# Who makes the sums of the activations' quarters, VectorE or GpSimd, in a kernel whose order a planner sets

## The chip, the cores and the metric

The kernel runs on one core of one Trainium2 chip. The metric is the device time of one execution in microseconds (us). The core's engines are called here as the profile calls them: PE (TensorE, matmuls; PEld is its weight load), DVE (VectorE), ACT (ScalarE), POOL (GpSimd) and SP (SyncE, which issues the DMA transfers).

## The reference

Eight batches of attention between 512 tokens and 32 states in 8 heads of 64, in both directions, give 512 + 32 rows of width 512 a batch. A feed-forward layer with a hard-swish follows on all 4352 rows. All arithmetic is fp32.

```python
scores = scale * x @ state.T;  a = softmax(scores);   xread = a @ state
scores2 = scale * state @ x.T; a2 = softmax(scores2); sread = a2 @ x
x = concat([xread, sread], axis=2)        # (8, 8, 544, 64) -> 4352 x 512
h = x @ w_in                              # 512 x 2048
g = h * clip(h + 3, 0, 6) / 6
out = g @ w_out                           # 2048 x 512
```

## The kernel before, in words

**Split products.** The PE multiplies in fp32r, which keeps fewer digits than fp32. An operand is therefore split into a high and a low half: ACT copies it into an fp32r tile (the high half, line 379), DVE subtracts that from the original (the low half, line 380), and each product is three matmuls (high by high, high by low, low by high).

**Units and steps.** The hidden width of 2048 is cut in 16 blocks `f` of 128. The work runs in two sweeps, blocks 0 to 7 and blocks 8 to 15. In each sweep there are nine units: one for the 512 tokens of each of the eight batches, and a ninth for all 256 state rows. A unit has eight steps, one a block. `first` (its matmuls stand on line 988, into a bank `ps_h`; there are two such banks) makes one block of `h`; ACT adds 3 and clips below (line 1159, tile `G`), DVE clips above and multiplies (line 1161). The first sweep's `second` multiplies that by `w_out` and adds up in four PSUM banks `acc`. Each unit also needs `wprime` (line 604), which folds a batch's states into `w_in`; its results are split as well (tiles `wp_hi`, `wp_lo`, at some units `raw`).

**Seven products in place of eight.** In the second sweep the units of batches 1 to 7 (units 10 to 16) run the second product by a seven-product scheme, in `seconds(k, t)`. The 512 tokens are two halves `q`, each two groups `r` of 128; the eight blocks are four pairs `p`, each two blocks `i`. For one `t`, which is one (q, p), the left operand is a 2 by 2 arrangement of quarters (i, r), each 128 x 128. Four sums of quarters are made (tile `g`, name `s_of(m)`): (0,1)+(1,1), (0,0)-(0,1), then the first less (0,0), and (1,0) less that. They are split into a pair of tiles `tmp` of 128 x 512; the four quarters themselves are split into `g_hi`, `g_lo` of 128 x 512. Seven products, of three matmuls each, go to the four banks on line 1075. Fifty-six `t` run so: 7 units of 8. `combine` makes the right operands' sums once, from `w_out`, on DVE. At the end of each half `q` the banks are put together: ACT and DVE evict them, and four additions (line 1098: two of 128 x 256 in the tile `tops`, two of 128 x 512 into `ot`) finish the output rows.

The names that the change touches are these two lines; `G_` puts an instruction on POOL, `V` on DVE, and the numbers are what the planner takes it to cost:

```python
SUMS, SUM_ENGINE, SUM_COST = G_, nc.gpsimd, 0.4
ADDS, ADD_ENGINE, ADD_COST = G_, nc.gpsimd, (0.7, 1.3)
```

**What sets the order.** Nothing is issued as the code meets it. Every instruction group is handed to `Plan` with its engine, a cost, and what it reads and writes. `Plan.order` then simulates all engines and the DMA queue with those costs and, among what is ready, takes the one with the lowest number in the table `RANKS`. A DMA counts as landed after its size over a rate, 1.4 us and a further allowance `late`. Each engine executes its list strictly in that order.

Of the kernel before, what the change touches and what calls it, by code (L numbers as in the profile page):

```python
# [10 lines left out]
F32 = mybir.dt.float32  # L11
# [268 lines left out]
def tile_state_attention_then_hardswish_ffn(  # L280
# [13 lines left out]
    P = 128  # L294
# [687 lines left out]
    def product(ps, terms, start=True, stop=True):  # L982
# [3 lines left out]
        for (ah, al), (bh, bl) in terms:  # L986
            for l, r in ((ah, bh), (ah, bl), (al, bh)):
                nc.tensor.matmul(ps, l, r, start=start and k == 0, stop=stop and k == n - 1)  # L988
                k += 1

    first_of = {}
    whole_of = {}

    def whole(k, p):

# [465 lines left out]
```

## Time and profile before

| | |
|---|---|
| median of 3 runs | 665.23 us (664.82 to 666.5) |
| profiled execution | 665.26 us, of which the profile's span is 663.5 us |
| PE busy | 642.4 us, 97% |
| DVE busy | 483.2 us, 73% |
| ACT busy | 337.3 us, 51% |
| POOL busy | 190.1 us, 29% |
| granted PE clock | full in the stretches from 0 to 640 us |

Busy is the time in which an engine executes at least one instruction. POOL's share is low only over the whole span: it does next to nothing until the seven-product units begin at about 395 us. Matmuls overlap one another, so one that is listed with 0.28 us can be followed by the next after 0.12 us.

### The profile page before, as it was taken

Reading aid. Unit: us, or ns where it says so; the run is one execution under the profiler, and the core shown is the slowest. Engines: PE = TensorE matmul, PEld = TensorE weight load, DVE = VectorE, ACT = ScalarE, POOL = GpSimd, SP = SyncE. Lnnn points to the kernel's source line nnn. Section 1 sums busy time; section 2 is a strip of 40 time slices with the busy share of each in tenths; the row PEclk is TensorE's granted clock in tenths of the full one; section 3 lists DMA queues with packets and bytes.
Section 4 is the critical chain, followed back from the end, with each engine's and each line's share of the span. In section 5 each row is a group of like instructions: output and inputs, shape, how many; then the busy total and the mean of one; then the engine's idle time right before and its main releaser. Section 6 shows DMA issues by size and latency. Waiting matters only on the chain.

```text
span 663.5 us, 11542 instructions
## 1 busy us (share of the span) xinstructions
PE 642.4 (97%) x4383; PEld 516.1 (78%) x4383; DVE 483.2 (73%) x799; ACT 337.3 (51%) x591; POOL 190.1 (29%) x287
## 2 busy tenths in 40 slices
PE   8999999999999999999999999999999999999997
PEld 7446776877777777777886788988888979889896
DVE  4989798988979668686589447666866577776753
ACT  4856445555545544535356336455555455545442
POOL 0000000000000000000000017777876588687732
PEclk9999999999999999999999999999999999999999
DMA  9975795867777549243013033232131312240012
GB/s 296 281 157 157 151 207 123 236 112 216 163 205 160 153 88 254 32 127 91 7 68 127 38 131 127 100 93 98 46 127 56 135 54 79 96 160 33 33 65 63
DMA packets 147007, 82.00 MB, mean 124 GB/s; under 512 B 124808, under 2 KB 134536, under 8 KB 144776
## 3 DMA queue, kind: packets, MB, share of 16 engines
q1 hardware_dynamic: 146808, 81.01, 44.7%
q8 instruction: 34, 0.56, 0.4%
q10 hardware_dynamic: 144, 0.26, 0.1%
q14 instruction: 21, 0.17, 0.1%
HBM read 50.84 MB, written 26.74 MB: 117 GB/s over the span
## 4 chain that ended last, share of the span: by engine, by line
PE 64%; POOL 11%; DVE 11%; ACT 4%; SPq 4%; DMA 3%; issue 3%; DVEq 0%; POOLq 0%; ACTq 0%
PE acc L988 23%; PE ps_h L988 22%; PE acc L1075 9%; POOL g L1045 9%; PE ps_s L604 2%; DVE tmp L380 2%; PE ps_s L988 2%; POOL ot L1098 2%; ACT tmp L379 2%; DMA raw<-in_moe_w_in_dram 2%; PE acc L1209 2%; SPq L917 1%; SPq L591 1%; DVE g_lo L380 1%; PE ps_h L604 1%
## 5 line engine op out<-in xcount | busy, mean ns | idle before, releaser
L1045 POOL TENSOR_TENSOR g<-G 128x128 f32<-128x128 f32 x112 | 67.8, 618 | 428.2 <-DVE G L1161 397.8
L988 PE MATMUL acc<-w_out_hi,g_hi 128*128 128x512 f32 x288 | 114.4, 397 | 0.0
L988 PE MATMUL acc<-w_out_hi,g_lo 128*128 128x512 f32 x288 | 112.2, 390 | 0.9 <-DVE g_lo L380 0.9
L1075 PE MATMUL acc<-w_out_hi,tmp 128*128 128x256 f32 x448 | 111.4, 286 | 1.7 <-DVE tmp L380 1.3
L988 PE MATMUL acc<-w_out_lo,g_hi 128*128 128x512 f32 x288 | 112.4, 390 | 0.0
L1174 ACT ACTIVATE g<-ps_h,three 128x512 f32<-128x512 f32 (+1 forms) x88 | 57.2, 650 | 78.4 <-PE ps_h L988 61.0
L988 PE MATMUL ps_h<-aT_hi,wp_hi 128*128 128x512 f32 (+1 forms) x232 | 85.8, 370 | 3.2 <-DVE wp_lo L380 1.7
L1075 PEld LDWEIGHTS acc<-w_out_hi,tmp 128*128 128x128 f32 x448 | 82.6, 191 | 7.0 <-issue 2.5
L988 PE MATMUL ps_h<-aT_lo,wp_hi 128*128 128x512 f32 (+1 forms) x232 | 83.9, 362 | 0.2 <-DVE aT_lo L380 0.2
L1176 DVE SCALAR_TENSOR_TENSOR g<-g,ps_h 128x512 f32<-128x512 f32 (+1 forms) x88 | 55.7, 635 | 39.0 <-ACT g L1174 38.2
L988 PE MATMUL ps_h<-aT_hi,wp_lo 128*128 128x512 f32 (+1 forms) x232 | 83.6, 360 | 0.0
L380 DVE TENSOR_TENSOR g_lo<-g,g_hi 128x512 fp32r<-128x512 f32 (+1 forms) x84 | 54.7, 655 | 21.9 <-ACT g_hi L379 20.2
L379 ACT CAST g_hi<-g 128x512 fp32r<-128x512 f32 (+1 forms) x84 | 48.5, 579 | 41.4 <-PE acc L988 30.9
L988 PEld LDWEIGHTS acc<-w_out_hi,g_hi 128*128 128x128 f32 x288 | 54.1, 188 | 19.4 <-issue 7.8
L380 DVE TENSOR_TENSOR tmp<-g,tmp 128x512 fp32r<-128x512 f32 x56 | 46.2, 833 | 28.8 <-ACT tmp L379 27.3
L988 PEld LDWEIGHTS acc<-w_out_hi,g_lo 128*128 128x128 f32 x288 | 54.1, 188 | 12.8 <-DVE g_lo L380 1.4
L1075 PE MATMUL acc<-w_out_lo,tmp 128*128 128x256 f32 x224 | 63.4, 283 | 0.0
L988 PEld LDWEIGHTS acc<-w_out_lo,g_hi 128*128 128x128 f32 x288 | 54.1, 188 | 10.9 <-DVE w_out_lo L496 0.3
L1159 ACT ACTIVATE G<-ps_h,three 128x512 f32<-128x512 f32 x56 | 38.4, 689 | 44.9 <-PE ps_h L988 44.7
L1161 DVE SCALAR_TENSOR_TENSOR G<-G,ps_h 128x512 f32<-128x512 f32 x56 | 37.9, 683 | 30.4 <-ACT G L1159 30.1
L379 ACT CAST tmp<-g 128x512 fp32r<-128x512 f32 x56 | 34.2, 619 | 47.1 <-POOL g L1045 45.8
L988 PEld LDWEIGHTS ps_h<-aT_hi,wp_hi 128*128 128x128 f32 x232 | 43.8, 189 | 13.9 <-DVE wp_lo L380 2.4
(152 smaller groups left out, 1304.0 us busy)
## 6 DMA issues: line engine op xcount, KB each, us to landing
part<-ot SPq DMA_DIRECT2D x8, 1024.0 KB, 5.0
ot<-part SPq DMA_DIRECT2D x8, 1024.0 KB, 6.2
raw<-in_x_dram SPq DMA_DIRECT2D x112, 64.0 KB, 2.9
xb<-in_x_dram SPq DMA_DIRECT2D x28, 256.0 KB, 4.3
out_dram<-ot SPq DMA_DIRECT2D x14, 512.0 KB, 3.2
raw<-in_moe_w_out_dram SPq DMA_DIRECT2D x11, 511.8 KB, 5.9
raw<-in_moe_w_in_dram SPq DMA_DIRECT2D x8, 511.0 KB, 4.5
raw<-raw SPq DMA_DIRECT2D x112, 32.0 KB, 2.0
```

The source lines that it names most:

```text
L379: S_(cost, rank, lambda: nc.scalar.copy(hi(), src()), reads, [writes[0]])
L380: V(cost, rank, lambda: nc.vector.tensor_tensor(lo(), src(), hi().bitcast(F32), op=ALU.subtract), [*reads, writes[0]], [writes[1]])
L604: nc.tensor.matmul(out[u][cols, :], made["stT", b][rows, cols], moving(q)[rows], start=True, stop=True,)
L988: nc.tensor.matmul(ps, l, r, start=start and k == 0, stop=stop and k == n - 1)
L1045: SUMS(SUM_COST, rank - 2.5, lambda m=m, a=a, b=b, op=op, of=of: SUM_ENGINE.tensor_tensor(s_of(m), of(a), of(b), op=op), g_keys + [(*s_key ...
L1075: nc.tensor.matmul(out, left(a, l), right(b, r), start=p == 0 and z == 0 and y == 0, stop=p == FPS // 2 - 1 and y == 2, skip_group_check=True)
L1098: add = lambda wide, out, a, b, reads, writes: ADDS(ADD_COST[wide], rank, lambda: ADD_ENGINE.tensor_tensor(out(), a(), b(), op=ALU.add), r ...
L1159: S_(0.68, n - 1.5, lambda: nc.scalar.activation(g(), bank(ps), AF.Relu, bias=three), [ps], [g_key], after)
L1161: V(0.63, n - 1.5, lambda: nc.vector.scalar_tensor_tensor(g(), g(), 6.0, bank(ps), op0=ALU.min, op1=ALU.mult), [ps], [g_key])
L1174: S_(cost + 0.05, rank, lambda: nc.scalar.activation(g(), bank(ps)[:, :width], AF.Relu, bias=three), [ps], [g_key])
L1176: V(cost, rank, lambda: nc.vector.scalar_tensor_tensor(g(), g(), 6.0, bank(ps)[:, :width], op0=ALU.min, op1=ALU.mult), [ps], [g_key])
L1209: nc.tensor.matmul(bank(acc), made["g_hi", n][:, js], plain_out[f][1](), start=opens, stop=closes)
```

## The change

The four sums of quarters move from POOL to DVE. The second of them, now (0,1) less (0,0), with the opposite sign, is written over the quarter (0,1), which no product uses by itself. It is then split along with the quarters, in the tile that already held a split of (0,1), so the sums' own tile has three parts instead of four and its split is 128 x 384 instead of 128 x 512. The split of the quarters now waits for that subtraction. The right operand gets the opposite sign too. POOL keeps the additions on the banks' results. The planner's costs are new for the sums and the additions, its allowance for DMA is 2.0 instead of 3.0, some loads may be issued earlier, and the table RANKS is new.

```diff
 RANKS = [int(k) for k in """
-159 160 158 211 208 311 209 59 207 58 232 60 233 55 226 57 234 205 206 54 56 309 215 231 307 567 308 219 214 306 216
...
-    def Q(rank, size, do, reads=(), writes=(), after=(), pieces=128, cost=0.46, late=3.0):
+    def Q(rank, size, do, reads=(), writes=(), after=(), pieces=128, cost=0.46, late=2.0):
...
-        for m, a, less in ((0, (0, 1), (0, 0)), (2, (1, 1), (0, 1)), (1, (1, 1), 0), (3, (1, 0), 1)):
+        for m, a, less in ((0, (0, 1), (0, 0)), (2, (0, 1), (1, 1)), (1, (1, 1), 0), (3, (1, 0), 1)):
...
-        s_all = lambda: get(s_key, lambda: gp.tile([P, S], F32, name="g"))
+        s_all = lambda: get(s_key, lambda: gp.tile([P, S], F32, name="g"))[:, : 3 * P]
         s_of = lambda m: s_all()[:, m * P : (m + 1) * P]
         for m, a, b, op, reads in (
-            (0, (0, 1), (1, 1), ALU.add, ()), (2, (0, 0), (0, 1), ALU.subtract, ()),
-            (1, 0, (0, 0), ALU.subtract, (0,)), (3, (1, 0), 1, ALU.subtract, (1,)),
+            (0, (0, 1), (1, 1), ALU.add, ()), ((0, 1), (0, 1), (0, 0), ALU.subtract, (0,)),
+            (1, 0, (0, 0), ALU.subtract, (0,)), (2, (1, 0), 1, ALU.subtract, (1,)),
         ):
             of = lambda c: s_of(c) if isinstance(c, int) else quarter(*c)
-            SUMS(SUM_COST, rank - 2.5, lambda m=m, a=a, b=b, op=op, of=of: SUM_ENGINE.tensor_tensor(
-                s_of(m), of(a), of(b), op=op), g_keys + [(*s_key, r) for r in reads], [(*s_key, m)])
-        s_keys = [(*s_key, m) for m in range(4)]
+            sum_of[k * FPS + t, m] = SUMS(SUM_COST, rank - 2.5, lambda m=m, a=a, b=b, op=op, of=of: SUM_ENGINE.tensor_tensor(
+                of(m), of(a), of(b), op=op), g_keys + [(*s_key, r) for r in reads],
+                [(*s_key, m)] if isinstance(m, int) else [("G", (k, p), "less", q)],
+                [sum_of[k * FPS + t - 1, m]] if (k * FPS + t - 1, m) in sum_of else [])
+        s_keys = [(*s_key, m) for m in range(3)]
...
         split(rank - 2, a_half["hi"], a_half["lo"], lambda: whole(k, p)[:, :, 2 * q * P : 2 * (q + 1) * P],
-              g_keys, a_keys)
-        split(rank - 1.5, s_half["hi"], s_half["lo"], s_all, s_keys, half_keys)
+              [*g_keys, ("G", (k, p), "less", q)], a_keys)
+        split(rank - 1.5, s_half["hi"], s_half["lo"], s_all, s_keys, half_keys, 0.5)
...
             (((0, 0), (0, 0)), (1, 1)),
-            ((2, 2),),
-            (((1, 0), (1, 0)), (3, (1, 1))),
+            (((0, 1), 2),),
+            (((1, 0), (1, 0)), (2, (1, 1))),
             (((1, 1), 3), (0, 0)),
...
-    SUMS, SUM_ENGINE, SUM_COST = G_, nc.gpsimd, 0.4
-    ADDS, ADD_ENGINE, ADD_COST = G_, nc.gpsimd, (0.7, 1.3)
+    SUMS, SUM_ENGINE, SUM_COST = V, nc.vector, 0.24
+    ADDS, ADD_ENGINE, ADD_COST = G_, nc.gpsimd, (0.85, 1.45)
...
-        first_of[n] = T(1.95 if plain(k, c) else 1.37 if b < B else 1.45, n, run, reads, [ps], after)
+        first_of[n] = T(1.95 if plain(k, c) else 1.37 if b < B else 1.45, n, run, reads, [ps],
+                        after + ([first_of[n - 3]] if n > 2 else []))
...
-            at(n - 2, sread_split, k, n - 3)
+            at(n - 2, lambda k=k, n=n: sread_split(k, n - 3, [first_of[n - FPS]]))
...
-            at(n - 5, lambda k=k, n=n: again(k, n - 6, [first_of[n - 6]]))
+            at(n - (10 if k == B + 1 else 5), lambda k=k, n=n: again(k, n - 6, [first_of[n - (11 if k == B + 1 else 6)]]))
```

The built programs have the same number of instructions on PE (3745), ACT (578) and SP (395). POOL goes from 292 to 68, DVE from 801 to 1025. On PE 336 matmuls change an operand (`tmp` for `g_hi` or `g_lo`), none its size.

The first place is POOL's list in the middle of the seven-product units, before the change, with the sums (line 1045) and the additions of one half's end (line 1098):

```order
L1045 TENSOR_TENSOR g<-G 128x128 x2
L1045 TENSOR_TENSOR g<-g,G 128x128
L1045 TENSOR_TENSOR g<-G,g 128x128
L1098 TENSOR_TENSOR tops<-tops 128x256
L1098 TENSOR_TENSOR ot<-ot,tops 128x512
L1098 TENSOR_TENSOR tops<-tops 128x256
L1098 TENSOR_TENSOR ot<-ot,tops 128x512
L1045 TENSOR_TENSOR g<-G 128x128 x3
L1045 TENSOR_TENSOR g<-g,G 128x128
L1045 TENSOR_TENSOR g<-G,g 128x128
```

A stretch of POOL's list after the change (the additions now stand on line 1100):

```order
L1100 TENSOR_TENSOR tops<-tops 128x256
L1100 TENSOR_TENSOR ot<-ot,tops 128x512
L1100 TENSOR_TENSOR tops<-tops 128x256
L1100 TENSOR_TENSOR ot<-ot,tops 128x512
L1100 TENSOR_TENSOR tops<-tops 128x256 x2
L1100 TENSOR_TENSOR ot<-ot,tops 128x512 x2
```

All sums are gone from it: what was queued behind additions is on another engine.

The second place is DVE's list before the change at unit 14, where the folded weights of that unit (`wp_lo` and `raw`, from `ps_h` and `ps_s`) are split behind the low halves of two sums (`tmp`):

```order
L1161 SCALAR_TENSOR_TENSOR G<-G,ps_h 128x512
L380 TENSOR_TENSOR tmp<-g,tmp 128x512
L1161 SCALAR_TENSOR_TENSOR G<-G,ps_h 128x512
L1092 SCALAR_TENSOR_TENSOR ot<-acc_4830,ot 128x512
L380 TENSOR_TENSOR g_lo<-G,g_hi 128x512
L380 TENSOR_TENSOR tmp<-g,tmp 128x512
L1095 SCALAR_TENSOR_TENSOR ot<-acc_4858,ot 128x256
L380 TENSOR_TENSOR wp_lo<-ps_h,wp_hi 128x512 x2
L380 TENSOR_TENSOR raw<-ps_s,raw 128x512 x2
L1161 SCALAR_TENSOR_TENSOR G<-G,ps_h 128x512 x2
```

The same place after the change (the clipping of `G` is now line 1164, the evictions lines 1094 and 1097; `G<-G` is the sum in place, `g<-G`, `g<-g,G` and `g<-G,g` are the other three):

```order
L1045 TENSOR_TENSOR g<-G 128x128
L1045 TENSOR_TENSOR G<-G 128x128
L380 TENSOR_TENSOR g_lo<-G,g_hi 128x512
L1045 TENSOR_TENSOR g<-g,G 128x128
L1045 TENSOR_TENSOR g<-G,g 128x128
L1094 SCALAR_TENSOR_TENSOR ot<-acc_5307,ot 128x512
L1094 SCALAR_TENSOR_TENSOR ot<-acc_5289,ot 128x512
L380 TENSOR_TENSOR tmp<-g,tmp 128x384
L380 TENSOR_TENSOR raw<-ps_h,raw 128x512
L380 TENSOR_TENSOR wp_lo<-ps_s,wp_hi 128x512
L380 TENSOR_TENSOR raw<-ps_h,raw 128x512
L380 TENSOR_TENSOR g_lo<-G,g_hi 128x512
```

The four sums of a `t` now stand in DVE's own list, and the low half `tmp` behind them is narrower; the weights' split still stands behind such a `tmp`.

## Rows read from the trace of the kernel before

**Rows 1.** Busy time by engine in stretches of the span, with granted clock, DMA share.

```profile
core 0: us, PE busy (x) PEld busy (x) DVE busy (x) ACT busy (x) POOL busy (x), PEclk, DMA share, GB/s
60.00:120.00 60.00, 58.49 (x466) 44.20 (x456) 50.49 (x90) 28.99 (x50) 0.00 (x0) 1.00 0.80 178
120.00:240.00 120.00, 119.80 (x767) 91.72 (x773) 98.91 (x177) 64.25 (x112) 0.00 (x0) 1.00 0.70 167
200.00:220.00 20.00, 20.00 (x112) 15.24 (x111) 18.74 (x36) 11.96 (x22) 0.00 (x0) 1.00 0.64 136
240.00:400.00 160.00, 158.25 (x1000) 124.80 (x985) 112.83 (x196) 74.78 (x126) 3.99 (x9) 1.00 0.35 95
400.00:640.00 240.00, 232.40 (x1698) 206.05 (x1697) 166.26 (x235) 125.22 (x221) 181.07 (x268) 1.00 0.26 90
```

**Rows 2.** PE's matmuls in order of time: start, duration; in brackets idle time, releaser.

```profile
414.02 0.39 PE L1075 MATMUL acc<-w_out_hi,tmp 128*128 128x256 f32 x1 [0.20 <-ACT tmp L379]
...
540.77 0.28 PE L1075 MATMUL acc<-w_out_lo,tmp 128*128 128x256 f32 x1
540.89 0.28 PE L1075 MATMUL acc<-w_out_hi,tmp 128*128 128x256 f32 x1
542.40 0.50 PE L988 MATMUL ps_h<-aT_hi,raw 128*128 128x512 f32 x1 [1.22 <-DVE wp_lo L380]
542.74 0.40 PE L988 MATMUL ps_h<-aT_lo,raw 128*128 128x512 f32 x1
542.97 0.39 PE L988 MATMUL ps_h<-aT_hi,raw 128*128 128x512 f32 x1
...
633.58 0.50 PE L988 MATMUL ps_s<-w_out_hi,g_lo 128*128 128x512 f32 x1 [0.36 <-DVE g_lo L380]
```

**Rows 3.** The chain that ended last, between 534 and 543 us.

```profile
538.89 0.89 POOL g L1045 x2
...
539.80 0.63 ACT tmp L379
...
541.06 0.68 DVE tmp L380
541.74 1.20 DVE wp_lo L380 x2
```

**Rows 4.** Waits between 400 and 640 us: total, times, longest.

```profile
ACT tmp L379 <- POOL g L1045: 45.6, 28, 3.7
```

**Rows 5.** POOL's groups between 400 and 640 us: busy us, mean ns, idle before.

```profile
L1045 POOL TENSOR_TENSOR g<-G 128x128 f32<-128x128 f32 x108 | 65.6, 619 | 34.6 <-DVE tmp L380 22.8 <-ACT g_hi L379 6.7 <-DVE G L1161 4.2
L1098 POOL TENSOR_TENSOR ot<-ot,tops 128x512 f32<-128x512 f32 x26 | 37.0, 1426 | 6.5 <-DVE ot L1095 5.3 <-POOL tops L1098 0.3
L1045 POOL TENSOR_TENSOR g<-g,G 128x128 f32<-128x128 f32 x54 | 30.8, 573 | 3.3
L1045 POOL TENSOR_TENSOR g<-G,g 128x128 f32<-128x128 f32 x54 | 29.7, 551 | 3.1
L1098 POOL TENSOR_TENSOR tops<-tops 128x256 f32<-128x256 f32 x26 | 22.1, 849 | 7.6 <-ACT tops L1088 6.0 <-ACT tops L1089 1.0
```

**Rows 6.** DVE's groups between 400 and 640 us.

```profile
L380 DVE TENSOR_TENSOR g_lo<-G,g_hi 128x512 fp32r<-128x512 f32 x54 | 46.6, 872 | 6.7 <-ACT g_hi L379 6.4
L380 DVE TENSOR_TENSOR tmp<-g,tmp 128x512 fp32r<-128x512 f32 x55 | 45.4, 833 | 28.8 <-ACT tmp L379 27.3 <-PE acc L1075 1.2
...
L1092 DVE SCALAR_TENSOR_TENSOR ot<-acc,ot 128x512 f32<-128x512 f32 x26 | 17.7, 685 | 3.3 <-PE acc L1075 3.1
...
L1095 DVE SCALAR_TENSOR_TENSOR ot<-acc,ot 128x256 f32<-128x256 f32 x13 | 5.5, 420 | 0.2
```

**Rows 7.** DVE's sums of the right operands (`combine`), in order of time.

```profile
337.33 1.55 DVE L1020 TENSOR_TENSOR raw<-raw 128x256 f32<-128x256 f32 x4
...
346.13 1.68 DVE L1020 TENSOR_TENSOR raw<-raw 128x256 f32<-128x256 f32 x4
```

**Rows 8.** An addition on POOL and a subtraction on DVE, in order of time.

```profile
488.75 1.62 POOL L1098 TENSOR_TENSOR ot<-ot,tops 128x512 f32<-128x512 f32 x1
...
489.14 1.78 DVE L380 TENSOR_TENSOR g_lo<-G,g_hi 128x512 fp32r<-128x512 f32 x1
```

More of the change, by code (lines that the diff above doesn't have):

```diff
@@ L471, in weight @@
         Q(load_rank, 524.288 * n, load, writes=[key], pieces=128 * n if kind == "out" else 512,
-          late=3.0 if k >= FPS else 0.0)
+          late=2.0 if k >= FPS else 0.0)
         lo = key + ("lo",)
@@ L529, in load_state @@
             return
-        plan.add("Q", 2.1, rank, load_blocks, (), [key], after, 140.0, 512, 3.0)
+        plan.add("Q", 2.1, rank, load_blocks, (), [key], after, 140.0, 512, 2.0)
     def turn_state(b, rank, after):
@@ L991, in tile_state_attention_then_hardswish_ffn @@
     first_of = {}
-    whole_of = {}
+    whole_of, sum_of = {}, {}
     def whole(k, p):
@@ L1050, in seconds @@
         s_half = {h: (lambda h=h: get(("tmp", (f"S_{h}", k, t)), lambda: att.tile(
-            [P, 4 * P], F32R, name="tmp", bufs=8))) for h in ("hi", "lo")}
+            [P, 4 * P], F32R, name="tmp", bufs=8))[:, : 3 * P]) for h in ("hi", "lo")}
         a_keys = [(f"g_{h}", ("A", k, t)) for h in ("hi", "lo")]
@@ L1273, in w_in_split, with sread_split @@
             [("wp", (k, c), "hi")], [("wp", (k, c), "lo")], after)
-    def sread_split(k, rank):
+    def sread_split(k, rank, after):
         a = who(k)
@@ L1280, in sread_split @@
         S_(1.2, rank, lambda: nc.scalar.copy(hi_lo["hi"](), sread_t),
-           [("sread", b) for b in range(B)], [("aT", a, "hi")])
+           [("sread", b) for b in range(B)], [("aT", a, "hi")], after)
         V(1.25, rank, lambda: nc.vector.tensor_tensor(
```

217 rows, old and new, of the table RANKS are left out of this document.

## The prediction, made before the changed kernel ran

> **What bounds the kernel now.** I read the busy time by stretch first [rows 1], because a change in the seven-product units can only be worth what is lost there. PE is the bound in every stretch: it is busy 232.40 of the 240 us from 400 to 640, in which all but the first steps of units 10 to 16 lie. So the kernel can gain no more there than PE stands still, and the second reading is what that is.
>
> The shown idle time is 240 - 232.40 = 7.60 us [rows 1]. It comes in 17 stops; the first, the last and one of the longest stand in [rows 2]. A stop costs more than its idle time, since the overlap of matmuls must build up again. From 540.89 to 542.74 two matmuls were started in 1.85 us; undisturbed they take 0.12 (540.77 to 540.89) and 0.23 (542.74 to 542.97), so 1.50 us were lost where 1.22 are shown [rows 2]. With 0.28 for each of 17 stops, 7.6 + 4.8 = 12.4 us are lost to PE in this stretch.
>
> The third reading is the chain of work behind such a stop [rows 3]. PE waited for `wp_lo` on DVE; DVE did that right behind two `tmp`, the low halves of sums; they had to wait for ACT's `tmp`, and that for POOL's sums, which ended at 539.78. In the list of DVE before the change, `wp_lo x2` stands behind `tmp` just so. The waits say that this is the rule: ACT waited 45.6 us in 28 waits for POOL's sums [rows 4], with DVE's list held up behind. POOL was busy 181.07 us of these 240 [rows 1]: 126.1 for the sums, 59.1 for the additions [rows 5] (the groups overlap a little). A sum took 551 to 619 ns where the planner counts 400, so the four of a `t` took 2 x 0.619 + 0.573 + 0.551 = 2.36 us instead of 1.6. The additions took 849 and 1426 ns where it counts 700 and 1300. The list was made for a faster POOL than the one it runs on.
>
> **What the change does, part by part.** PE executes the same matmuls in the same sizes, so all terms are waits.
>
> *POOL.* The sums leave: 126 us of the 181. About 59 us of additions stay. No `tmp` waits for POOL any more.
>
> *DVE, what is added.* 224 sums of 128 x 128, in 56 sets of four; DVE has made none of this shape from these tiles. The nearest row is `combine`, which makes four such sums, 128 x 256, one behind another: 1.68 us where two wait for the one before them, 1.55 in another set [rows 7]. Between 256 and 512 columns a DVE instruction goes from 420 to 685 ns [rows 6], so 128 columns are 0.133 us and a set costs 1.68 - 4 x 0.133 = 1.15 us, or 1.02 by the other row. I take 1.15, since two or three sums of a set need the one before: 56 x 1.15 = 64 us (57 to 64). A set is thus 1.2 us shorter than POOL's 2.36, and there is no hand-over between engines.
>
> *DVE, what is removed.* `tmp` is 128 columns narrower: 56 x 0.133 = 7.4 us. And DVE has been held up by POOL: `tmp` and `g_lo` from `G`, which read two tiles of SBUF, take 833 and 872 ns; the eviction of the same size, which reads PSUM, 685 [rows 6]. That is (0.148 + 0.187) x 56 = 18.8 us. How much of it stays depends on what POOL still does. By proportion: POOL's busy time falls to 59/181, and DVE's time in instructions with two SBUF inputs grows from 92 us (46.6 + 45.4) to 92 + 64 - 7 = 149, so 18.8 x 0.33 x 1.6 = 10 us. The bounds are nothing and, if every addition's whole time were to fall on DVE, 59 us. I take 10, because it is scaled from the same two kinds of instruction.
>
> That such a collision can cost an addition's whole time is seen at 489.14: DVE's `g_lo` started 0.39 us into an addition on POOL, which ended at 490.37, and itself ended at 490.92, 0.55 us later; it took 1.78 us instead of 0.69 [rows 8]. The Trainium skill, page "SBUF — State Buffer", section "Who interferes with whom", states this as a rule: a DVE instruction with two SBUF inputs and a GpSimd instruction that reads SBUF exclude each other for the whole instruction. This case's row agrees. The rule speaks against the change, as it puts 224 more instructions of that kind on DVE and leaves the longest ones on POOL; what that can cost is the first rival.
>
> *DVE, sum.* 166.3 + 64 - 7.4 - 18.8 + 10 = 214 us of work in a stretch that took 240: DVE goes from 69% to some 92% of what is left of it.
>
> *ACT.* Its `tmp` copy gets narrower; it has 125 us of 240 [rows 1] and gains room. Its copy `g_hi` now waits for the sum in place as well. Behind it in ACT's list stand the clips that free `ps_h` for PE. The wait is at most the set's 1.15 us, and PE has two banks; I put it at nothing, and at up to 1 us a unit, 7 us, if that cover fails.
>
> *PE's waits that remain.* For DVE this full the rows of the first sweep are the yardstick, where POOL does nothing. From 60 to 400 us DVE was busy 50.49 + 98.91 + 112.83 = 262 of 340 us, and PE idle 1.51 + 0.20 + 1.75 = 3.46 us; from 200 to 220 DVE was at 18.74 of 20 and PE not idle at all [rows 1]. Per 240 us that is 2.4 us idle, and with the ratio 12.4 / 7.6 of lost to shown idle time 4.0 us lost.
>
> *The rest.* The rule that a first step follows the one three before it, the later split of the state rows and the earlier loads of unit 10 move work that PE doesn't wait for: they cost nothing as long as the DMA engines have room (share 0.35 and 0.26 from 240 on [rows 1]). Without it, a late load is a stop of a microsecond or so. The shorter DMA allowance and the new table reorder the first sweep too, where 3.46 x 12.4 / 7.6 = 5.6 us are lost from 60 to 400; I take no change there, with half of it, 2.8 us, either way.
>
> *The sum.* 12.4 - 4.0 = 8.4 us less. The profiled execution took 665.26 us (span 663.5 and 1.8 around it), the median is 665.23; so 665.2 - 8.4 = **656.8**, told as 657 us.
>
> **Rivals.**
>
> *DVE becomes the bound (slower).* Place: units 10 to 16, wherever an addition on POOL meets a sum or a split on DVE. If the additions' whole 59 us fall on DVE, its work is 166.3 + 64 - 7.4 - 18.8 + 59 = 263 us; the stretch can't be shorter than that, so it takes 23 us more: 688. It decides from 240 - 204 = 36 us on, or 0.7 us for each of the 52 additions there. For it: the 1.09 us lost in [rows 8]. Against it: a large part of DVE's list reads PSUM, and in one stretch DVE was 94% busy at no cost to PE [rows 1]. Likely 674 to 688. Chance 0.12.
>
> *The gain is given back elsewhere (no change).* The planner now takes a transfer to land 1 us earlier than it did. If in each of the eight units of the first sweep after the first, where the DMA share is 0.80 and 0.70 [rows 1], one load comes later than planned, that is 8 x 1 us, and the kernel is back at 665. The `g_hi` wait above, at its 7 us, gives 664 and is the same case. For it: PE's idle time is higher from 60 to 120, where DMA is fullest. Against it: from 120 to 240 it is 0.20 us at a share of 0.70. Chance 0.13.
>
> *PE waits no more.* As from 120 to 240 us, where DVE was at 82% [rows 1]: 0.2 us idle a 120, or 0.7 lost in 240. Gain 11.7, time 653.5. Against it: POOL's additions were not there. Chance 0.17.
>
> **How the numbers follow.** The forecast, most of the stops gone, has 0.58; its own range is 654 to 660.5. The range of 8 in 10 reaches down to the third rival with the first sweep's 2.8 us (651) and up to the second with some 2 us on top (667), and leaves out the first rival and a little below 651. About 0.3%, 2 us, is what a measurement of this kernel can tell from no change. Faster by more than that are the forecast and the third rival, with a little of the second: 0.77; slower is the first, with a little of the second: 0.13; the same: 0.10.
>
> **What would show it.** Right: POOL busy about 60 us in the whole seven-product stretch; no wait of ACT for POOL's sums; sets of four sums on DVE of about 1.1 us; `tmp` at 0.56 to 0.62 us; DVE busy about 90% of the stretch, which is some 8 us shorter; PE's idle time there 2 to 3 us. Wrong: DVE without gaps there and PE waiting for it (first rival), with `g_lo` near 1 us in the mean; PE's idle time before 400 us grown by what the later stretch gains (second); sums of 0.3 us and more each, with DVE's own waits between them, which would add up to 70 us and more.

## The result, and the profile after

The changed kernel takes 656.66 us (median of 4 runs, 656.3 to 658.88), the kernel before beside it 665.43 (4 runs, 664.82 to 666.5): a ratio of 0.9873, 95% interval 0.9848 to 0.9899. The forecast was 657.0. The span of the profiled execution fell from 663.5 to 654.2 us.

From the page of the changed kernel, the busy time of each engine (part 1) and the shares of the chain that ended last (part 4):

```profile
PE 638.1 (98%) x4383; PEld 514.9 (79%) x4383; DVE 530.1 (81%) x1023; ACT 331.9 (51%) x591; POOL 63.3 (10%) x63
...
PE 79%; DVE 11%; SPq 4%; DMA 3%; issue 2%; ACT 1%; DVEq 0%; ACTq 0%
```

POOL is off the chain; on the page before it had 11% of it, and PE 64%. Busy time by stretch, the rows that answer to [rows 1]; the last stretch is cut at 23.2 us from the span's end. Of before, the two rows that [rows 1] lacks, the first stretch and the last one cut at the same place (640.3):

```profile
0.00:60.00 60.00, 54.69 (x358) 32.54 (x362) 47.25 (x89) 38.61 (x73) 0.96 (x7) 1.00 0.80 225
...
400.00:640.30 240.30, 232.70 (x1700) 206.35 (x1699) 166.26 (x235) 125.22 (x221) 181.07 (x268) 1.00 0.26 90
```

And after:

```profile
core 0: us, PE busy (x) PEld busy (x) DVE busy (x) ACT busy (x) POOL busy (x), PEclk, DMA share, GB/s
0.00:60.00 60.00, 56.21 (x341) 33.68 (x342) 47.79 (x90) 39.25 (x74) 0.95 (x7) 1.00 0.80 225
60.00:120.00 60.00, 56.77 (x467) 42.53 (x466) 49.02 (x89) 28.59 (x49) 0.00 (x0) 1.00 0.81 171
120.00:240.00 120.00, 118.99 (x756) 90.83 (x755) 99.15 (x177) 65.09 (x113) 0.00 (x0) 1.00 0.71 171
240.00:400.00 160.00, 159.80 (x1017) 127.80 (x1016) 114.70 (x205) 75.30 (x127) 0.00 (x0) 1.00 0.35 101
400.00:631.00 231.00, 227.86 (x1688) 203.44 (x1687) 211.47 (x449) 118.17 (x219) 58.26 (x52) 1.00 0.25 89
```

Up to 400 us PE is idle 8.23 us, before 8.77. From 400 on the same end is reached 9.3 us sooner: PE is idle 3.14 us, in 6 stops, where it was idle 7.60 in 17 [rows 2], and its busy time is 4.8 us less (232.70 to 227.86), though over the span it executes the same 4383 matmuls (168 of them, not 336, with another operand). That second half is lost overlap behind each stop and work that now stands before 400 us. The traces hold all matmuls, so this work can be counted. In the last stretch 313 matmuls of 128x512 and 1194 of 128x256 start before the change, 307 and 1188 after it. At the 0.23 and 0.12 us by which undisturbed ones follow each other, the difference is 2.1 us, which nine matmuls of 128x512 more before 400 us make up.

The sum of PE's idle time up to 400 us hides a shift. From 60 to 240 us it grew from 1.71 to 4.24 us; from 0 to 60 and from 240 to 400 us it fell by 3.07 us. One new stop stands behind a transfer: PE waits for `wp_lo`, which DVE makes right behind a transpose of rows of `x`; DVE had stood still for 1.38 us until their load landed at 140.35:

```profile
142.40 0.47 PE L988 MATMUL ps_h<-aT_hi,wp_hi 128*128 128x512 f32 x1 [0.96 <-DVE wp_lo L380]
```

Groups on DVE from 400 to 631 us (answer to [rows 6]; L1045 are the four sums), and POOL's there (answer to [rows 5]):

```profile
L380 DVE TENSOR_TENSOR g_lo<-G,g_hi 128x512 fp32r<-128x512 f32 x56 | 40.5, 729 | 2.1 <-ACT g_hi L379 2.0
L380 DVE TENSOR_TENSOR tmp<-g,tmp 128x384 fp32r<-128x384 f32 x54 | 34.1, 638 | 2.2 <-ACT tmp L379 1.4 <-PE acc L1077 0.4
...
L1045 DVE TENSOR_TENSOR g<-G 128x128 f32<-128x128 f32 x54 | 20.1, 378 | 0.8
L1045 DVE TENSOR_TENSOR G<-G 128x128 f32<-128x128 f32 x54 | 19.8, 374 | 0.5
L1045 DVE TENSOR_TENSOR g<-g,G 128x128 f32<-128x128 f32 x54 | 19.5, 369 | 0.7
...
L1045 DVE TENSOR_TENSOR g<-G,g 128x128 f32<-128x128 f32 x54 | 17.1, 326 | 0.9
```

```profile
L1100 POOL TENSOR_TENSOR ot<-ot,tops 128x512 f32<-128x512 f32 x26 | 36.4, 1402 | 30.2 <-DVE ot L1097 19.7 <-DVE ot L1094 9.2 <-DVE tmp L380 0.6
L1100 POOL TENSOR_TENSOR tops<-tops 128x256 f32<-128x256 f32 x26 | 22.0, 846 | 536.6 <-DVE g L1045 415.9 <-ACT tops L1090 113.2 <-ACT tops L1091 7.0
```

The splits got shorter than in [rows 6], but the sums take 326 to 378 ns each, 1.45 us a set. ACT's waits (answer to [rows 4]) have moved from POOL to DVE; they add up to 40.7 us, where those for POOL's sums were 45.6, and no stop of PE ends with ACT any more:

```profile
ACT tmp L379 <- DVE g L1045: 24.9, 20, 3.7
...
ACT g_hi L379 <- DVE G L1045: 15.8, 7, 3.3
```

The longest stop left is at 458.06 us. In order of time, PE, then DVE and POOL just before (start, duration; in brackets idle time and releaser; answers to [rows 2] and [rows 8]):

```profile
456.64 0.28 PE L1077 MATMUL acc<-w_out_lo,g_hi 128*128 128x256 f32 x1
458.06 0.39 PE L1077 MATMUL acc<-w_out_hi,g_lo 128*128 128x256 f32 x1 [1.14 <-DVE g_lo L380]
```

```profile
452.28 0.72 DVE L1045 TENSOR_TENSOR g<-g,G 128x128 f32<-128x128 f32 x1
453.04 1.33 DVE L1045 TENSOR_TENSOR g<-G,g 128x128 f32<-128x128 f32 x1
454.30 0.83 DVE L1045 TENSOR_TENSOR G<-G 128x128 f32<-128x128 f32 x1
455.05 0.67 DVE L1164 SCALAR_TENSOR_TENSOR G<-G,ps_h 128x512 f32<-128x512 f32 x1
455.64 1.11 DVE L380 TENSOR_TENSOR tmp<-g,tmp 128x384 fp32r<-128x384 f32 x1
...
457.33 0.68 DVE L380 TENSOR_TENSOR g_lo<-G,g_hi 128x512 fp32r<-128x512 f32 x1
```

```profile
452.12 0.74 POOL L1100 TENSOR_TENSOR tops<-tops 128x256 f32<-128x256 f32 x1 [9.14 <-ACT tops L1090]
452.93 1.29 POOL L1100 TENSOR_TENSOR ot<-ot,tops 128x512 f32<-128x512 f32 x1
454.18 0.79 POOL L1100 TENSOR_TENSOR tops<-tops 128x256 f32<-128x256 f32 x1
455.05 1.29 POOL L1100 TENSOR_TENSOR ot<-ot,tops 128x512 f32<-128x512 f32 x1
```

Four additions run one after another, and each of DVE's instructions that reads two tiles of SBUF ends just after one of them: 454.37 after 454.22, 456.75 after 456.34. Against 0.288 us for a sum and 0.553 for `tmp` where POOL does nothing (experiments below), the three sums and the `tmp` lose 2.57 us; the clip `G`, which reads PSUM, loses nothing. PE then waits 1.14 us for `g_lo`, which stands behind them. Each of the other five stops has an addition and a DVE instruction of about twice its length in the six microseconds before it; before the one of 0.55 us at 522.38 a sum took 1.38 us beside an addition.

One thing in the text ahead needs a correction: the second list of DVE that is shown there as the same place after the change is the weights' split of the next unit, at 502 us in the trace. At the one that answers to the first list, at 468.8 us, the weights' split stands behind two `tmp` as before, so the reading holds.

### The profile page after: what moved, and what is told of

Read it like the earlier page. It is cut to its first block, busy times and chain, and to the rows that moved or that the text cites. A ratio compares the mean times of both kernels' runs of the same rounds, so it can differ in the third digit from the quotient of the medians.

```text
span 654.2 us, 11536 instructions
## 1 busy us (share of the span) xinstructions
PE 638.1 (98%) x4383; PEld 514.9 (79%) x4383; DVE 530.1 (81%) x1023; ACT 331.9 (51%) x591; POOL 63.3 (10%) x63
## 4 chain that ended last, share of the span: by engine, by line
PE 79%; DVE 11%; SPq 4%; DMA 3%; issue 2%; ACT 1%; DVEq 0%; ACTq 0%
PE ps_h L988 26%; PE acc L988 25%; PE acc L1077 18%; PE ps_s L604 3%; PE acc L1212 2%; DVE g_lo L380 2%; SPq L591 2%; PE ps_s L988 2%; PE ps_h L604 1%; PE ps_h L1143 1%; SPq L559 1%; DVE g L1045 1%; DVE tmp L380 1%; DMA raw<-in_moe_w_in_dram 1%; DMA raw<-in_x_dram 1%
## 5 line engine op out<-in xcount | busy, mean ns | idle before, releaser
L1077 PE MATMUL acc<-w_out_hi,tmp 128*128 128x256 f32 x336 | 88.0, 283 | 0.0
L1100 POOL TENSOR_TENSOR tops<-tops 128x256 f32<-128x256 f32 x28 | 23.5, 838 | 549.9 <-DVE g L1045 415.9
L1077 PE MATMUL acc<-w_out_hi,g_lo 128*128 128x256 f32 x224 | 63.8, 285 | 1.7 <-DVE g_lo L380 1.7
L1077 PEld LDWEIGHTS acc<-w_out_hi,tmp 128*128 128x128 f32 x336 | 64.4, 192 | 0.1
L1077 PE MATMUL acc<-w_out_hi,g_hi 128*128 128x256 f32 x224 | 64.0, 286 | 0.3 <-DVE ot L1094 0.3
L1077 PE MATMUL acc<-w_out_lo,g_hi 128*128 128x256 f32 x224 | 63.4, 283 | 0.0
L988 PEld LDWEIGHTS ps_h<-aT_hi,wp_lo 128*128 128x128 f32 x232 | 43.8, 189 | 6.9
```

What stands on the lines that cost most here:

```text
L1077: nc.tensor.matmul(out, left(a, l), right(b, r), start=p == 0 and z == 0 and y == 0, stop=p == FPS // 2 - 1 and y == 2, skip_group_check=True)
L1100: add = lambda wide, out, a, b, reads, writes: ADDS(ADD_COST[wide], rank, lambda: ADD_ENGINE.tensor_tensor(out(), a(), b(), op=ALU.add), r ...
```

## The experiments

All but two, the truer costs and the second sum out of place, keep the order of one of the two kernels' lists. That is possible because the order follows from the planner's costs and table and from what each group reads and writes, not from the engine object that executes a group.

**The engine alone.** The list of before; its sums are executed by DVE where the list has them for POOL.

```diff
-    SUMS, SUM_ENGINE, SUM_COST = G_, nc.gpsimd, 0.4
+    SUMS, SUM_ENGINE, SUM_COST = G_, nc.vector, 0.4
```

> The kernel before with its own list of work, in which only the engine of the four sums is DVE instead of POOL; nothing is planned anew, no sum is in place, tmp stays 512 wide. Theory A (the gain is that POOL's sums came late and held up ACT's and DVE's lists): most of the 9 us is there, 657 to 661 us, although the list was made without these sums on DVE. Theory B (the gain is the new plan and its truer costs): nothing is gained, 665 us, or it is slower, up to 675, as DVE's list was not made for 64 us more.

Measured: 665.97 us, before 666.42; ratio 1.0001 (0.9983 to 1.002). The sums leave POOL, and nothing is gained. The worst stop of its trace, on PE, then DVE and POOL:

```profile
581.20 0.28 PE L1075 MATMUL acc<-w_out_hi,tmp 128*128 128x256 f32 x1
584.13 0.50 PE L988 MATMUL ps_h<-aT_hi,wp_hi 128*128 128x512 f32 x1 [2.65 <-DVE wp_lo L380]
```

```profile
579.82 1.78 DVE L380 TENSOR_TENSOR g_lo<-G,g_hi 128x512 fp32r<-128x512 f32 x1
581.52 1.75 DVE L380 TENSOR_TENSOR tmp<-g,tmp 128x512 fp32r<-128x512 f32 x1
583.19 0.28 DVE L1045 TENSOR_TENSOR g<-G 128x128 f32<-128x128 f32 x1
583.39 0.68 DVE L380 TENSOR_TENSOR wp_lo<-ps_h,wp_hi 128x512 fp32r<-128x512 f32 x1
```

```profile
579.31 3.41 POOL L1098 TENSOR_TENSOR ot<-ot,tops 128x512 f32<-128x512 f32 x2
```

`wp_lo`, for which PE waits, stands behind two splits that two additions hold up. From 579.31 to 583.27 is 3.96 us; two additions of 1.29 and two splits of 0.685 one after another are 3.95. That is what they take when they run in turn. The rule of the Trainium skill named ahead ("SBUF — State Buffer", "Who interferes with whom": the two exclude each other for a whole instruction) would have it so, and the sum of the four agrees. The moments of the hand-over don't show as cleanly: the `tmp` before them, from 579.11 to 579.90, overlaps the first addition by 0.59 us and is only 0.1 us longer than undisturbed.

**The list alone.** The list of after; its sums are executed by POOL.

```diff
-    SUMS, SUM_ENGINE, SUM_COST = V, nc.vector, 0.24
+    SUMS, SUM_ENGINE, SUM_COST = V, nc.gpsimd, 0.24
```

> The changed kernel with its own list, in which only the engine of the sums is POOL again; the one in place, the narrower tmp and the new plan stay. Theory A: the sums take 2.3 us a set again where the list expects 1 us, and PE stops as often as before or more: 664 to 675 us. Theory B: the new list keeps most of its gain: 656 to 659.

Measured: 666.16 us; 1.0002 (0.9985 to 1.0018). Neither half of the change gives anything alone. Theory A has the number here and missed the one of the run before, theory B the other way round, so neither holds as it was put.

**Truer costs.** The kernel before with its table, planned with what its sums and additions took in [rows 5].

```diff
-    SUMS, SUM_ENGINE, SUM_COST = G_, nc.gpsimd, 0.4
-    ADDS, ADD_ENGINE, ADD_COST = G_, nc.gpsimd, (0.7, 1.3)
+    SUMS, SUM_ENGINE, SUM_COST = G_, nc.gpsimd, 0.62
+    ADDS, ADD_ENGINE, ADD_COST = G_, nc.gpsimd, (0.85, 1.45)
```

> The kernel before, sums on POOL, with the same table RANKS, planned with the costs that POOL has on the chip (0.62 for a sum, 0.85 and 1.45 for the additions, instead of 0.4, 0.7 and 1.3). Theory A (POOL's time itself): no more than a third of the gain, 662 to 667 us. Theory B (the list was made for a faster POOL): 656 to 660.

Measured: 675.12 us; 1.0134 (1.0112 to 1.0157). Both expectations missed. ACT's wait for POOL's sums fell from 45.6 [rows 4] to 18.0 us, and the kernel got slower. So the sum of that wait is no measure of what PE loses.

```profile
ACT tmp L379 <- POOL g L1045: 18.0, 17, 4.4
```

```profile
634.13 0.58 PE L1075 MATMUL acc<-w_out_hi,tmp 128*128 128x256 f32 x1 [3.69 <-ACT tmp L379]
```

It does not clear the sums, though. This longest stop of 3.69 us stands behind one of those waits: the chain before it has an addition of 2.20 us on POOL, then three sums there, then ACT's `tmp`. The granted clock also fell three times, as in the last section. The order is another one here, so the run speaks for a table that goes with the costs it was found for, but does not price POOL's time.

**The second sum out of place**, and `tmp` 512 wide again, in nearly the list of after. Three more lines change with these: the sums' tile has four parts again, the split of `tmp` reads the second sum too, and the product takes it from `tmp`.

```diff
-                of(m), of(a), of(b), op=op), g_keys + [(*s_key, r) for r in reads],
+                s_of(m) if isinstance(m, int) else s_of(3), of(a), of(b), op=op), g_keys + [(*s_key, r) for r in reads],
-            [P, 4 * P], F32R, name="tmp", bufs=8))[:, : 3 * P]) for h in ("hi", "lo")}
+            [P, 4 * P], F32R, name="tmp", bufs=8))) for h in ("hi", "lo")}
```

> The changed kernel and its list, in which the second sum has its own place again, so that tmp is 512 wide on ACT and DVE. By the sum of the prediction DVE gets 56 x 0.133 = 7.4 us more and is at some 95% of the seven-product units. If DVE is not the bound there: 656.5 to 658 us. If it is: 660 to 664, most of the 7.4 us.

Measured: 660.11 us; 0.9922 (0.9898 to 0.9946). The split of `tmp` has one more thing to wait for, and the planner ordered the work anew with it: ACT's list differs from that of after from 465 us on, DVE's from 480 and PE's from 532. So the 3.4 us between the two kernels, of the 8.8, are the sum in place together with these differences. DVE has 218.32 us of work from 400 on instead of 211.47, 6.9 us more where 7.4 were expected.

**No additions**, in the list of after. The additions on the banks' results are left out, so part of units 10 to 16's output is missing.

```diff
-        add = lambda wide, out, a, b, reads, writes: ADDS(ADD_COST[wide], rank, lambda: ADD_ENGINE.tensor_tensor(
-            out(), a(), b(), op=ALU.add), reads, writes)
+        add = lambda wide, out, a, b, reads, writes: ADDS(ADD_COST[wide], rank, lambda: None, reads, writes)
```

> The changed kernel and its list without POOL's additions on the banks' results, which leaves part of the output out; POOL then does nothing in the seven-product units. It prices what POOL still costs: the hold-ups of DVE (put at 10 us of DVE's time in the prediction) and any wait for POOL. If PE's remaining stops come from them: 653 to 655 us. If not: 656 to 657. In both cases g_lo and tmp should fall to 0.69 and 0.55 us, a sum to 0.28 to 0.30.

Measured: 651.34 us, before 666.12; 0.9777 (0.9752 to 0.9802), below both expectations. Its last stretch, and DVE's groups in it:

```profile
400.00:625.70 225.70, 225.70 (x1690) 203.46 (x1689) 190.07 (x451) 119.64 (x220) 0.00 (x0) 1.00 0.26 91
```

```profile
L380 DVE TENSOR_TENSOR g_lo<-G,g_hi 128x512 fp32r<-128x512 f32 x56 | 38.2, 687 | 4.8 <-ACT g_hi L379 4.4
...
L380 DVE TENSOR_TENSOR tmp<-g,tmp 128x384 fp32r<-128x384 f32 x54 | 29.4, 553 | 4.2 <-PE acc L1077 2.1 <-ACT tmp L379 1.8
...
L1045 DVE TENSOR_TENSOR g<-G 128x128 f32<-128x128 f32 x54 | 15.3, 288 | 0.8
```

PE does not stop once: 225.7 us is what its matmuls take there. POOL's 58 us of additions cost DVE 211.47 - 190.07 = 21.4 us and the kernel 656.66 - 651.34 = 5.3.

**The first sum made twice**, in the list of after: 56 more instructions on DVE.

```diff
+            def make(m=m, a=a, b=b, op=op, of=of):
+                for _ in range(2 if m in TWICE else 1):
+                    SUM_ENGINE.tensor_tensor(of(m), of(a), of(b), op=op)
...
+    TWICE = (0,)
```

> The changed kernel and its list with the first of the four sums made twice: 56 more instructions of 128 x 128 on DVE, 0.2 to 0.32 us each, 11 to 18 us in the seven-product units (some 6% of them), where DVE is 92% busy. If DVE has that much room: 657 to 659 us. If DVE is the bound: 665 to 672.

Measured: 669.62 us; 1.0049 (1.0031 to 1.0066). DVE's work from 400 on is 228.63 us, 17 more than after, and the kernel takes 13 us more.

**Three sums made twice**, the same edit with `TWICE = (0, 1, 2)`: 168 more instructions.

> The changed kernel and its list with three of the four sums made twice: 168 more instructions on DVE, 34 to 54 us. DVE's work, 211 us of 231, then passes the stretch: 245 to 265 us, so 670 to 690 us. Faster than 668 would say that DVE's busy time in the profile is more than what it needs.

Measured: 700.39 us; 1.0509 (1.0486 to 1.0532). That is slower than the expected 670 to 690. DVE has 258.59 us of work, 47 more; 44 us of them show. So the list of after has no room for more work on DVE at this place, as long as POOL adds beside it. Whether DVE's total does that is not shown by these two runs: a sum made twice also comes later to ACT and to the splits behind it, and DVE still stands idle for 16 us of the stretch in either run (245.1 - 228.63; 274.6 - 258.59).

**The engine alone, without additions.** The first experiment with the additions left out as above.

> The list of before with the sums executed by VectorE, and the 56 additions on GpSimd left out (so part of each output row of units 10 to 16 is missing). With the additions this list gave 665.97 us, no gain. Theory A (what eats the gain there is the additions colliding with DVE's sums and splits): the stops go as they did in the list of after without additions (651.3 us), so 651 to 655 us, PE's idle time in the stretch under 1 us. Theory B (what eats it is the order of the list, made for sums on another engine): the stops stay without the additions, 660 to 664 us, with PE's idle time of 4 us and more, though DVE has only some 187 us of work.

Measured: 657.98 us, before 665.47; 0.9888 (0.9867 to 0.9909). Between the two theories: 8.0 us were the additions, and 6.6 us to the same without additions in the list of after (651.34) remain with the list, the width of `tmp` among it.

**Before without additions.** The same lines left out of the kernel before; its sums stay on POOL.

> The kernel before, sums on GpSimd, with the 56 additions on GpSimd left out (so part of each output row of units 10 to 16 is missing). GpSimd then has 126 us or less of work in 240. If the additions, queued ahead of sums and slowing DVE, are the most of before's stops: 653 to 657 us, and ACT's waits for GpSimd's sums fall from 45.6 us to under 15. If it is the sums themselves, 2.4 us a set where the planner counts 1.6: 660 to 664 us, with 30 us and more of these waits left.

Measured: 656.92 us; 0.9881 (0.9855 to 0.9906). The last stretch, and ACT's wait in it:

```profile
400.00:631.30 231.30, 229.75 (x1701) 205.84 (x1700) 155.88 (x236) 125.92 (x221) 124.15 (x216) 1.00 0.27 93
```

```profile
ACT tmp L379 <- POOL g L1045: 33.0, 26, 2.7
```

Of ACT's waits for POOL's sums 72% are still there, and PE is idle 1.55 us, in 5 stops. The time agrees with the first expectation, the waits with the second: in this list the sums' slowness by itself costs PE little.

**The small additions on DVE**, in the list of after; the 128x512 ones stay on POOL.

```diff
-    ADDS, ADD_ENGINE, ADD_COST = G_, nc.gpsimd, (0.85, 1.45)
+    ADDS, ADD_ENGINE, ADD_COST = G_, (nc.vector, nc.gpsimd), (0.85, 1.45)
```

> The list of after, with the 128x256 additions executed by VectorE and the 128x512 ones by GpSimd as before. DVE gets 26 x 0.42 = 11 us more work in the stretch and is spared these additions' share of the contention, 22 of 58 us of GpSimd's time or 8 us of 21. If DVE's total is what counts: 211.5 + 3 us, 657 to 660 us. If collisions at bad moments count for more than the total, 654 to 656 us.

Measured: 655.59 us; 0.9865 (0.9839 to 0.9891). In the second expectation, but with no clear difference from after.

**All additions on DVE**, in the list of after.

```diff
-    ADDS, ADD_ENGINE, ADD_COST = G_, nc.gpsimd, (0.85, 1.45)
+    ADDS, ADD_ENGINE, ADD_COST = G_, nc.vector, (0.85, 1.45)
```

> The list of after, with all additions executed by VectorE; GpSimd has nothing to do in the stretch. DVE gets 26 x 0.42 + 26 x 0.69 = 29 us more and is spared 21 us of contention: 211.5 + 8 = 220 us. If DVE's total is what counts: by the slope of the doubled sums (13 us of time for 17 us of work) 6 us more, 661 to 664 us. If contention costs more than DVE's busy time shows: 654 to 657 us.

Measured: 653.47 us; 0.9829 (0.9805 to 0.9853), the fastest complete kernel here and just below the second expectation. Its interval and that of after touch by 0.0005, but they were timed in different runs against before; the profile shows where the rest went. The last stretch, and the additions on DVE:

```profile
400.00:628.10 228.10, 227.76 (x1694) 204.28 (x1693) 212.40 (x503) 119.41 (x221) 0.00 (x0) 1.00 0.25 90
```

```profile
L1100 DVE TENSOR_TENSOR ot<-ot,tops 128x512 f32<-128x512 f32 x26 | 17.8, 685 | 0.0
...
L1100 DVE TENSOR_TENSOR tops<-tops 128x256 f32<-128x256 f32 x26 | 10.9, 420 | 0.6 <-ACT tops L1090 0.4
```

DVE is busy 212.40 us, as after (211.47), in a stretch 2.9 us shorter: 93%. Yet PE is idle 0.34 us, not 3.14. So the stops left in after don't come from DVE's total but from POOL's additions beside it, which hold up several of its instructions in a row, as at 452 to 457 us.

**The additions alone moved.** The same edit in the kernel before; its sums stay on POOL.

```diff
-    ADDS, ADD_ENGINE, ADD_COST = G_, nc.gpsimd, (0.7, 1.3)
+    ADDS, ADD_ENGINE, ADD_COST = G_, nc.vector, (0.7, 1.3)
```

> The kernel before with its list; the sums stay on GpSimd and the 56 additions are executed by VectorE. Theory C (what costs the time in before is GpSimd's additions, which hold up DVE and the sums behind them): about as without additions, 656.9 us, a little more for the 29 us on DVE, 656 to 660 us. Theory D (the list is made for additions on GpSimd; DVE's own list is held up behind them, as with the sums moved alone): 664 to 668 us.

Measured: 665.75 us, before 666.03; 0.9992 (0.9967 to 1.0018), as theory D has it. In the list of before, additions cost 9 us on either engine. The longest stop of the last stretch, on PE, then DVE:

```profile
477.38 0.50 PE L988 MATMUL ps_h<-aT_hi,wp_hi 128*128 128x512 f32 x1 [1.79 <-DVE wp_lo L380]
```

```profile
474.36 0.68 DVE L1098 TENSOR_TENSOR tops<-tops 128x256 f32<-128x256 f32 x1
...
476.01 0.71 DVE L1098 TENSOR_TENSOR ot<-ot,tops 128x512 f32<-128x512 f32 x1
476.64 1.27 DVE L380 TENSOR_TENSOR wp_lo<-ps_h,wp_hi 128x512 fp32r<-128x512 f32 x2
```

## Why the prediction was right, and where its reasons were not

The medians of the runs, by who makes the sums in which list, and where the additions are:

| | additions on POOL | on DVE | left out |
|---|---|---|---|
| list of before, sums on POOL | 665.4 (before) | 665.8 | 656.9 |
| list of before, sums on DVE | 666.0 | | 658.0 |
| list of after, sums on POOL | 666.2 | | |
| list of after, sums on DVE | 656.7 (after) | 653.5 | 651.3 |

**What PE lost.** The step held within its size: most of the gain is idle time and lost overlap of PE from 400 us on. How much, follows from the floor, the time that the matmuls of the stretch take without a stop. In the list of after without additions that is 225.7 us for 308 matmuls of 128x512 and 1188 of 128x256. By the counts given with the result it is 225.5 us for after and 227.6 for before. So after lost 231.0 - 225.5 = 5.5 us, where 4.0 was forecast, and before 240.3 - 227.6 = 12.7 (forecast 12.4). The stops are worth 7.2 of the 9.3 us in the profile, where 8.4 was forecast. The other 2.1 us are the matmuls that the new order has ahead of the 400 us mark, for which nothing was forecast. One error takes back most of the other: that the time came out within 0.3 us of the forecast is in part luck.

**Why it stood still.** This step failed. The prediction put the stops down to ACT's waits for POOL's sums, "the rule". Those waits can stay at 33 us and the stops are nearly gone (before without additions). The sums can leave POOL and nothing is gained (the engine alone). What most of the stops need are the additions: without them PE is idle 1.55, 2.48 and 0 us in the three kernels that leave them out, with the sums on either engine. How they do it shows at single stops. On POOL they hold up DVE's splits and sums (579.31 and 452 to 457 us above; in before itself the addition of [rows 8], behind which PE stops for 1.10 us at 491.57), and they stand ahead of sums in POOL's list. On DVE they stand in its list, and in the list of before DVE then reaches `wp_lo` late (477.38). Which of these costs how much in before was not tried apart. Moving the sums alone does not take that away. The gain needs the new list as well, which was put at nothing for this stretch: with sums on DVE, the list and the narrower `tmp` together are 666.0 - 656.7 = 9.3 us, of which the sum in place is some 3.4, with the reservation made there. Which part of the list gives the other 6 (the table, the costs, the DMA allowance, the rule on first steps, the earlier loads) was not tried apart. The engine counts only with that list: in it, sums on POOL cost 666.2 - 656.7 = 9.5 us, in the list of before nothing.

**DVE's work.** 211.5 us against 214, from two terms that were wrong in opposite ways. DVE without contention has 190 us, not 204. A sum without contention is 0.288 us, and all sums (line L1045) take 56 us of DVE's time, not 64; that is near the lower bound, 57, that the second row of [rows 7] gave. The other 6 us are in the rest of its work, 134 us where 166.3 - 7.4 - 18.8 = 140 was taken. The durations of these instructions add up about as forecast, to 151 us against 178 before; but where DVE's instructions follow each other at once their records overlap, and busy time counts the overlap once. The contention that remains was put at 10 us and is 21. Its scaling failed: it went by DVE's time in two-input instructions. By that scaling the splits were to lose 18.8 x 0.33 = 6.2 us, and they lose (0.042 x 56) + (0.085 x 54) = 6.9; the sums were to lose the other 3.8 and lose 54 x (0.090 + 0.087 + 0.082 + 0.038) = 16. In the mean a sum of 0.29 us loses as much (0.07 us) as a split of 0.55 or 0.69 (0.06). By count instead of time the term would have been 6.2 x (112 + 224) / 112 = 18.6 us. So one sign of being wrong came true: sums of 0.3 us and more that add up to over 70, namely 72.1 us. It was the additions that stretched them, not waits of DVE between them.

**`tmp` narrower.** 686 ns (the engine alone, without additions) to 553 without contention: 0.133 us an instruction, as worked out from [rows 6].

**ACT.** The wait of `g_hi` for the sum in place was to be at most 1.15 us; it is up to 3.3, 15.8 us in all. No cost to PE shows: no stop after ends with ACT, and in the 2.5 us before each of the six DVE had no gap of more than 0.05 us.

**Before 400 us** the new order gained 2.1 us by the count of matmuls, 0.5 of it idle time, within the 2.8 either way.

**The rivals.** The first, DVE as the bound, was nearer than its chance says. Its mechanism is what makes the longest stop after, its price 21 of the 36 us from which it was to decide; 17 us more of work on DVE (the first sum twice) were enough to lose the whole gain, and 47 more show almost in full, with the reservation made there. The second, the gain given back elsewhere, came in part: PE's idle time from 60 to 240 us grew by 2.5 us, 0.96 of it at a stop behind a load; the stretches before and behind made up for it. The third had PE's waits gone at 653.5 us, and what spoke against it was that POOL adds in this stretch; with the additions off POOL the kernel takes 653.47.

## What to carry to other kernels

The waits that a profile sums up are not what the bound engine loses: take one suspect away whole, and look at the bound engine's stops, before naming the cause. Where two engines hold each other up, count the instructions that can meet and not only their time: here short ones lost as much, in the mean, as long ones. And an engine that was 93% busy with nothing to disturb it served better here than one at 91% whose work was held up in clusters. An order made by a planner belongs to the costs and engines that it was made for, and neither half of such a change shows what the whole is worth.

## What the runs showed of the hardware

PE's granted clock fell behind some long stops. In the kernel with the engine alone changed, behind the 2.65 us at 584.13, and in the one with the additions alone moved, behind the 1.79 us at 477.38, these are the stretches of 4 us:

```profile
580.00:584.00 4.00, 1.48 (x13) 1.27 (x11) 4.00 (x5) 1.65 (x4) 2.72 (x2) 1.00 0.00 0
584.00:588.00 4.00, 3.87 (x15) 3.46 (x16) 3.86 (x11) 1.31 (x3) 0.00 (x0) 0.63 0.31 75
588.00:592.00 4.00, 4.00 (x33) 4.00 (x33) 2.44 (x8) 1.32 (x4) 0.00 (x0) 0.94 0.86 291
```

```profile
476.00:480.00 4.00, 2.62 (x7) 2.10 (x8) 3.71 (x6) 0.01 (x1) 1.83 (x4) 0.73 0.02 4
480.00:484.00 4.00, 4.00 (x25) 3.59 (x25) 1.96 (x3) 2.52 (x4) 0.00 (x0) 0.85 0.67 200
```

0.63 and 0.94, or 0.73 and 0.85, are means over time at 2.4 GHz and time at 1.2. Each fall cost (0.37 + 0.06) x 4 or (0.27 + 0.15) x 4 = 1.7 us, on top of the stop. The length of the stop alone does not decide it: in the kernel with three sums made twice, stops of 1.81 us at 521.29 and 1.74 us at 647.51 left the clock at 1.00.
